# Attention weights of the first half batch kept in float32 and transposed on TensorE, with v scaled on GpSimd, two weight tiles loaded early and more slack in the plan

## Chip, cores and metric

One core of a Trainium2 chip runs the whole program. The metric is the device time of one execution in microseconds; lower is better. The inputs are four batches of eight heads, 576 rows and 64 columns for q, k and v, a number tau, and four weight matrices, all float32.

## What is computed

```python
scores = scale * np.matmul(q, k.transpose(0, 1, 3, 2))
thresh = np.max(scores, axis=-1, keepdims=True) - tau
scores = np.where(scores >= thresh, scores, -1000000000.0)
scores = scores - np.max(scores, axis=-1, keepdims=True)
attn = np.exp(scores)
attn = attn / (np.sum(attn, axis=-1, keepdims=True) + 1e-09)
attn_out = np.matmul(attn, v)                     # (4, 8, 576, 64)
x = attn_out.transpose(0, 2, 1, 3).reshape(2304, 512)
h = x @ w1_in;  x = (h * np.clip(h + 3, 0, 6) / 6) @ w1_out
h = x @ w2_in;  out = (h - np.tanh(h)) @ w2_out   # hidden width 2048
```

## The kernel before, in words

**The order.** Nothing is issued where it is written. Each step is a `Task` with an engine, an estimated duration and a due time (`key`), recorded with `add`; buffers are `Buf`s of a `Ring`, from which the dependences follow. `Plan.issue` then plays the estimates through and issues, on each engine, the ready task with the smallest due time; `slack` makes a task ready later than its estimate. So every engine has a fixed list, worked off in order, and a changed estimate or due time moves neighbours in all lists.

**Attention.** A unit is one head's 128 query rows against all 576 keys (`softmax`, line 577 on). There are 144 units: per batch 16 in a first half (`g` = 0, row chunks 0 and 1 of each head), then 16 and four units of left-over rows. A unit is four score products on TensorE (128x288, line 577), the row maximum on VectorE (582), the exponential on ScalarE (584), the threshold (587 or 590) and the masking on VectorE (593), which leaves the unnormalised weights `e` in float32. Two units of a head make a pair. For a pair, ScalarE copies `e` to float16 (`pp`, 598), GpSimd writes the rest that float16 lost beside it (602), SP's queue sends one transposing DMA of 18 blocks (`pt`, 605), and `weighted` multiplies on TensorE: 14 float16 products of 65 columns per unit with v (628), and ScalarE takes the result (635). Column 65 of v holds ones, so the row sum comes along. v itself is scaled to a power of two and split into two float16 parts in `v_round` (525 to 543: ScalarE twice more, TensorE once, VectorE three small steps, GpSimd). `k_round` and `q_round` transpose k and q on TensorE and split them.

**First layer.** Its first half of hidden columns runs beside attention, per half batch: `x_round` normalises and transposes, `layer1` multiplies (`mm3`, line 388, and line 734). Each weight matrix is loaded in tiles of 512 KB by `load_w`, and each tile is split into a high and a low part: absolute value on ScalarE (358), four VectorE steps (a clamp, 361, then 363, 366, 369), a copy on ScalarE (376) and a subtraction on GpSimd (378). For the 16 tiles of this first half (`WA`) the working buffer `wu` of these steps is a PSUM tile `m`; for the 48 tiles of the other halves (`weights`) it is in SBUF. The PSUM ring `R_m` (two tiles) also holds the products of `layer1`.

**After attention.** The second half of the first layer, then the second layer over nine blocks of 256 rows (`hidden`). In the second layer's first two blocks GpSimd forms the low part of each gated tile (701), between the subtractions of the weight tiles of its second half (378).

## Time and profile before

| | us |
|---|---|
| runs: median (lowest to highest) of three | 1147.84 (1145.71 to 1150.57) |
| profiled execution, its time | 1146.78 |
| its span | 1144.7 |
| TensorE busy in the span | 1073.2 (94%) |
| VectorE | 718.4 (63%) |
| ScalarE | 616.5 (54%) |
| GpSimd | 419.0 (37%) |

The span is what the profiler sees of the execution; its own time is 2.1 us longer. The shares are averages over stages that differ, so the rows further down split the span into stretches. Engines are named PE (TensorE), DVE (VectorE), ACT (ScalarE), POOL (GpSimd) and SP in them, L and a number is the line of the kernel, `out<-in` are the tiles, and PEclk is TensorE's granted clock as a share of 2.4 GHz.

### The profile page before, as it was taken

Reading aid. Unit: us, or ns where it says so; the run is one execution under the profiler, and the core shown is the slowest. Engines: PE = TensorE matmul, PEld = TensorE weight load, DVE = VectorE, ACT = ScalarE, POOL = GpSimd, SP = SyncE. Lnnn points to the kernel's source line nnn. Section 1 sums busy time; section 2 is a strip of 40 time slices with the busy share of each in tenths; the row PEclk is TensorE's granted clock in tenths of the full one; section 3 lists DMA queues with packets and bytes.
Section 4 is the critical chain, followed back from the end, with each engine's and each line's share of the span. In section 5 each row is a group of like instructions: output and inputs, shape, how many; then the busy total and the mean of one; then the engine's idle time right before and its main releaser. Section 6 shows DMA issues by size and latency. Waiting matters only on the chain.

```text
span 1144.7 us, 23228 instructions
## 1 busy us (share of the span) xinstructions
PE 1073.2 (94%) x9104; PEld 1002.1 (88%) x9104; DVE 718.4 (63%) x1365; ACT 616.5 (54%) x1268; POOL 419.0 (37%) x420
## 2 busy tenths in 40 slices
PE   5668899999999999889999999989999999999998
PEld 4557788998999899889999999978999999999997
DVE  6889887678777867587865663995323333333232
ACT  6868888689677867445544443544323323323222
POOL 3666767667656765652412210465200000000000
PEclk8668899999999999999999999999999999999999
DMA  7889678777977787778633430241100000000000
GB/s 186 180 190 230 131 183 156 173 148 188 164 168 144 167 155 129 210 198 282 184 93 94 129 94 1 76 131 33 38 1 19 1 19 19 1 19 20 1 20 19
DMA packets 257454, 125.77 MB, mean 110 GB/s; under 512 B 200257, under 2 KB 250945, under 8 KB 257345
## 3 DMA queue, kind: packets, MB, share of 16 engines
q1 hardware_dynamic: 247296, 114.72, 43.0%
q0 software_dynamic: 9504, 9.44, 3.6%
q8 instruction: 72, 1.18, 0.4%
q14 instruction: 38, 0.30, 0.1%
q10 hardware_dynamic: 544, 0.13, 0.1%
HBM read 62.92 MB, written 18.87 MB: 71 GB/s over the span
## 4 chain that ended last, share of the span: by engine, by line
PE 74%; DVE 8%; issue 5%; ACT 5%; POOL 3%; DMA 3%; SPq 0%; POOLq 0%; DVEq 0%; ACTq 0%
PE ya L388 24%; PE m L388 18%; PE h L388 12%; PE s L577 7%; PE m L734 6%; PE tp L628 5%; DVE e L593 2%; PE tp L460 2%; POOL bi L378 1%; DVE z L582 1%; ACT e L584 1%; POOL g L701 1%; DMA pt<-pp 1%; DMA st<-in_moe_w_in_dram 1%; DVE st L369 1%
## 5 line engine op out<-in xcount | busy, mean ns | idle before, releaser
L602 POOL TENSOR_TENSOR pp<-e,pp 128x128 f16<-128x128 f32 (+3 forms) x160 | 185.4, 1179 | 119.3 <-ACT pp L598 58.3
L698 ACT ACTIVATE g<-t 128x256 fp32r<-128x256 f32 x216 | 90.0, 417 | 103.8 <-DVE t L905 78.2
L582 DVE TENSOR_REDUCE z<-s 128x1 f32<-128x576 f32 x144 | 108.2, 753 | 53.3 <-PE s L577 52.4
L701 DVE TENSOR_TENSOR g<-t,g 128x256 fp32r<-128x256 f32 x184 | 92.9, 505 | 71.9 <-PE ya L388 44.6
L593 DVE SCALAR_TENSOR_TENSOR e<-s,z,e 128x576 f32<-128x576 f32 x144 | 116.1, 811 | 15.6 <-ACT e L584 9.9
L388 PE MATMUL m<-xT,ai 128*128 128x256 f32 (+1 forms) x768 | 121.7, 304 | 3.7 <-DVE t L693 2.5
L577 PE MATMUL s<-ks,q 128*128 128x288 f32 x512 | 105.2, 334 | 17.2 <-DVE e L593 16.5
L388 PE MATMUL ya<-ao,g 128*128 128x512 f32 x432 | 113.7, 396 | 5.8 <-POOL g L701 4.8
L388 PE MATMUL ya<-g,bo 128*128 128x256 f32 x864 | 116.1, 283 | 2.0 <-DVE g L701 1.9
L584 ACT ACTIVATE e<-s,z 128x576 f32<-128x576 f32 x144 | 105.4, 738 | 23.3 <-DVE z L582 18.3
L388 PE MATMUL h<-x,bi 128*128 128x256 f32 x864 | 115.4, 283 | 0.1
L388 PE MATMUL m<-x,bi 128*128 128x256 f32 x864 | 115.1, 283 | 0.0
L388 PEld LDWEIGHTS h<-x,bi 128*128 128x128 f32 x864 | 111.0, 191 | 3.3 <-POOL bi L378 0.3
L388 PEld LDWEIGHTS m<-x,bi 128*128 128x128 f32 x864 | 111.0, 191 | 3.0
L388 PEld LDWEIGHTS m<-xT,ai 128*128 128x128 f32 x768 | 107.9, 192 | 6.0 <-DVE t L693 3.5
L388 PEld LDWEIGHTS ya<-g,bo 128*128 128x128 f32 x864 | 108.9, 192 | 2.8 <-DVE g L701 2.5
L388 PE MATMUL ya<-bo,g 128*128 128x512 f32 x432 | 111.2, 393 | 0.0
L577 PEld LDWEIGHTS s<-ks,q 128*128 128x128 f32 x512 | 81.7, 210 | 24.4 <-issue 9.3
L628 PE MATMUL tp<-vt,pt 128*128 128x65 f16 (+1 forms) x2240 | 87.9, 199 | 8.1 <-DMA pt<-pp 4.5
L388 PEld LDWEIGHTS ya<-ao,g 128*128 128x128 f32 x432 | 75.9, 189 | 21.1 <-POOL g L701 7.8
L628 PEld LDWEIGHTS <-pt 128*128 128x128 f16 (+1 forms) x2240 | 79.7, 104 | 16.3 <-DMA pt<-pp 6.5
L905 DVE TENSOR_TENSOR t<-h,t 128x256 f32<-128x256 f32 x72 | 30.4, 423 | 98.8 <-ACT t L903 98.8
(101 smaller groups left out, 1825.2 us busy)
## 6 DMA issues: line engine op xcount, KB each, us to landing
st<-in_moe_w_in_dram SPq DMA_DIRECT2D x32, 512.0 KB, 3.9
st<-in_moe_w_out_dram SPq DMA_DIRECT2D x32, 512.0 KB, 4.0
x<-xs POOLq DMA_DIRECT2D x18, 512.0 KB, 5.4
xs<-xT SPq DMA_DIRECT2D x8, 640.0 KB, 4.8
y<-ys SPq DMA_DIRECT2D x9, 512.0 KB, 8.9
kr<-in_k_dram SPq DMA_DIRECT2D x16, 256.0 KB, 3.1
vr<-in_v_dram SPq DMA_DIRECT2D x16, 256.0 KB, 3.6
xs<-xT SPq DMA_DIRECT2D x8, 512.0 KB, 4.5
```

The source lines that it names most:

```text
L388: nc.tensor.matmul(ps, l[a], r[b], start=first and t == 0 and i == 0, stop=last and t == 2 and i == n - 1,)
L460: nc.tensor.transpose(ps[:, o:o + w], s.rearrange("p r d -> p (r d)"), ident[p0:p0 + w, p0:p0 + w])
L577: nc.tensor.matmul(ps.t[:, half, 0:SH], l, ks[:, half * SH:(half + 1) * SH], start=i == 0, stop=i == len(ops) - 1,)
L582: add("dve", 0.69, key, lambda: nc.vector.tensor_reduce(out=z.t[:, 0:1], in_=s(), axis=AX.XY, op=ALU.max, negate=True), r=[ps], w=[z])
L584: exp = add("act", 0.66, key, lambda: nc.scalar.activation(out=ex(), in_=s(), func=ACTF.Exp, bias=z.t[:, 0:1]), r=[ps, z], w=[e])
L593: add("dve", 0.74, key, lambda: nc.vector.scalar_tensor_tensor(out=ex(), in0=s(), scalar=z.t[:, 1:2], in1=ex(), op0=ALU.is_ge, op1=ALU.mul ...
L602: add("pool", t_pool(w * (src.stop - src.start)), key, lambda src=src, dst=dst: nc.gpsimd.tensor_tensor(out=pp.t[:, 0:w, dst], in0=e.t[:, ...
L628: nc.tensor.matmul(pv.t[0:m, w_ * (D + 1):(w_ + 1) * (D + 1)], pt.t[:, n, blk, rows], vv, start=o == 0, stop=o == len(ops) - 1)
L698: hi = add("act", t_act(n, sbuf=True), key, lambda: nc.scalar.activation(out=gh(), in_=t(), func=ACTF.Copy), r=[bt], w=[bh])
L701: add(low, t_pool(n) if low == "pool" else t_dve(n), key, lambda: eng.tensor_tensor(out=gl(), in0=t(), in1=gh().bitcast(F32), op=ALU.subtr ...
L734: prev = [add("pe", t_mm(n, 1), kd, lambda p=p, l=l, r=r, m=m, s=s, ps=ps: nc.tensor.matmul(ps.t[:, 0:n], W["o", m].t[:, l, s], r[m].t[:, ...
L905: add("dve", t_dve(n), key, lambda: nc.vector.tensor_tensor(out=s_(), in0=p(), in1=s_(), op=ALU.subtract), r=[ps, t], w=[t])
```

## The change

For the first half of batch 0 (`plain`, 16 of 144 units), the weights `e` stay float32. TensorE transposes them in four blocks per unit into a PSUM tile of `R_m`, and the 64 left-over columns of both units of a pair into another tile; ScalarE copies both to SBUF, in the memory that `pt` and `pp` had. `weighted32` multiplies them, five float32 products per unit, with v as loaded (`load_v32`, three loads per pair of heads and a column of ones; the memory is that of weight tiles not yet needed). These eight pairs have no float16 copy, no GpSimd subtraction and no transposing DMA. The split of v of batch 0 is due only before its second half. For all v, the scaling by the power of two goes from ScalarE to GpSimd.

In `load_w` the absolute value is always written to SBUF, and the clamp is done there; for the first eight tiles (`low`) by GpSimd. The next step reads SBUF and writes the PSUM tile, which is therefore taken later. The first two tiles are asked for on ScalarE's queue without slack. k is due one unit later (`LK`), the tiles of the second layer's second half every 4 us in place of 3 (`W2S`), and the split steps of the later tiles get slacks of 0.1 to 0.3 us.

```diff
-    LK, LQ, LV, LD = 5, 3, 1, 4
+    LK, LQ, LV, LD = 4, 3, 1, 4
+    CB, CC, CD = 0.1, 0.3, 0.2
-    W2B, W2S = 6.0, 3.0
+    W2B, W2S = 6.0, 4.0
+    NCL = 8
...
-        wst, wu, W = R_st.new(), (scratch or R_wu).new(), R_w[name, kind, m].new()
+        wst, wu, W = R_st.new(), R_wu.new(), R_w[name, kind, m].new()
+        sc = scratch.new() if scratch else wu
+        mid = lambda dt: sc.t.bitcast(dt)
+        eng, sync = ("act", nc.scalar) if queue else ("dma", nc.sync)
...
+        def clamp():
+            (nc.gpsimd if low else nc.vector).tensor_scalar(
+                out=part(F32), in0=part(F32), scalar1=TINY, scalar2=HUGE, op0=ALU.max, op1=ALU.min)
...
+        if low:
+            add("pool", t_pool(DM), key + 3, clamp, r=[wu], w=[wu], slack=cs)
+        else:
+            add("dve", 0.5, key + 3, clamp, r=[wu], w=[wu], slack=cs)
         steps = [
-            lambda: nc.vector.tensor_scalar(
-                out=part(F32), in0=part(F32), scalar1=TINY, scalar2=HUGE, op0=ALU.max, op1=ALU.min),
             lambda: nc.vector.tensor_scalar(
-                out=part(I32), in0=part(I32), scalar1=3, scalar2=0x3FFFFFF8,
+                out=mid(I32), in0=part(I32), scalar1=3, scalar2=0x3FFFFFF8,
...
-        add("act", t_act(N, sbuf=True, scalars=True), key, lambda: nc.scalar.activation(
-            out=raw(), in_=raw(), func=ACTF.Copy, scale=sv.t[:, 2 * j:2 * j + 1]), r=[vr, sv], w=[vr])
+        add("pool", t_pool(N), key, lambda: nc.gpsimd.tensor_scalar(
+            out=raw(), in0=raw(), scalar1=sv.t[:, 2 * j:2 * j + 1], scalar2=None, op0=ALU.mult), r=[vr, sv], w=[vr])
...
-        if u == us[-1]:
+        if plain(b, g):
+            transpose32(u, key, e, pp, pt, n, len(us))
+        elif u == us[-1]:
...
+    def transpose32(u, key, e, pp, pt, n, count):
+        tp = R_m.new()
+        def tr():
+            for i in range(NC):
+                nc.tensor.transpose(tp.t[:, i * 128:(i + 1) * 128], e.t[:, n, i * 128:(i + 1) * 128], ident)
+        add("pe", NC * 0.11, key, tr, r=[e], w=[tp])
+        add("act", t_act(SM), key, lambda: nc.scalar.activation(
+            out=blocks32(pt)[:, n].rearrange("p k n -> p (k n)"), in_=tp.t, func=ACTF.Copy), r=[tp], w=[pt])
+        if n == count - 1:
+            tl = R_tp.new()
+            def left():
+                for i in range(count):
+                    nc.tensor.transpose(tl.t[0:LF, i * 128:(i + 1) * 128], e.t[:, i, SM:S], ident)
+            add("pe", count * 0.11, key, left, r=[e], w=[tl])
+            add("act", t_act(count * 128), key, lambda: nc.scalar.activation(
+                out=left32(pp), in_=tl.t[0:LF, 0:count * 128].rearrange("p (u n) -> p u n", u=count),
+                func=ACTF.Copy), r=[tl], w=[pp])
+    def weighted32(u, key):
...
+                for i, cb in enumerate(ORDER):
+                    nc.tensor.matmul(out, blocks32(pt)[:, n, i, :], vv[:, h % 2, cb, :], start=i == 0, stop=False)
+                nc.tensor.matmul(out, left32(pp)[:, n, :], vv[0:LF, h % 2, NC, :], start=False, stop=True)
...
-                rounds.append((u - LV, ("v", b, j)))
+                rounds.append((first_unit[b, 1, j] - LV if plain(b, g) else u - LV, ("v", b, j)))
...
-                    "a", kind, m, w1_in if kind == "i" else w1_out, 0, T0 + STEP * (W0 + WS * n + WO * (kind == "o")), 0.8, slack=ST, scratch=R_m, cs=CS)
+                    "a", kind, m, w1_in if kind == "i" else w1_out, 0, T0 + STEP * (W0 + WS * n + WO * (kind == "o")), 0.8, slack=ST if n > 1 else 0.0, scratch=R_m, cs=CS, queue=n < 2, low=n < NCL)
```

**TensorE, the first pair of units.** Before, the first products with v (`vt`, `pt`) follow the scores (`s`) of eight units and the transposes of left-over q rows:

```order
L577 MATMUL s<-ks,q 128x288 x8
L476 MATMUL tp<-ident,left 64x64 x2
L460 MATMUL tp<-ident,left 128x64 x2
L577 MATMUL s<-ks,q 128x288 x8
L628 LDWEIGHTS pt
L628 MATMUL tp<-vt_94,pt 128x65
```

Now (`m<-ident,e` and the 64-row `tp<-ident,e` are the new transposes, `v_126` is v as loaded):

```order
L609 MATMUL s<-ks,q 128x288 x4
L668 MATMUL tp<-ident,e 64x128 x2
L658 MATMUL m<-ident,e 128x128 x4
L686 MATMUL tp<-v_126,pt 128x65 x4
L687 MATMUL tp<-v_126,pp 128x65
L686 MATMUL tp<-v_126,pt 128x65 x4
L687 MATMUL tp<-v_126,pp 128x65
L609 MATMUL s<-ks,q 128x288 x4
```

The 28 pairs of a weight load and a product are ten products, the transposes stand between the scores, and the first products follow the scores of four units, the last of which is the first row here.

**VectorE, the first weight tile.** Before, its clamp (361) and shift (363) work in the PSUM tile `m`, behind three small steps for v:

```order
L531 TENSOR_SCALAR vs<-tp 128x1
L533 TENSOR_SCALAR vs<-vs 128x1
L536 RECIPROCAL sv<-vs 128x2
L485 TENSOR_TENSOR ks<-tp,ks 64x2x64
L361 TENSOR_SCALAR m<-m 128x512
L593 SCALAR_TENSOR_TENSOR e<-s,z,e 128x576
L363 TENSOR_SCALAR m<-m 128x512
```

Now the shift (376) reads `wu` in SBUF and comes right behind the first maximum:

```order
L614 TENSOR_REDUCE z<-s 128x1
L376 TENSOR_SCALAR m<-wu 128x512
L517 TENSOR_TENSOR ks<-tp,ks 64x2x256 x2
L625 SCALAR_TENSOR_TENSOR e<-s,z,e 128x576
L614 TENSOR_REDUCE z<-s 128x1
L517 TENSOR_TENSOR ks<-tp,ks 64x2x64
L379 SCALAR_TENSOR_TENSOR m<-st,m 128x512
```

The clamp of this tile has left VectorE's list, and its other three steps stand 16 to 18 places earlier.

**GpSimd, second layer.** Before, from the first weight tile (`bi`) of the second half, with the low parts `g`:

```order
L378 TENSOR_TENSOR bo_11069<-st,bo_11069 128x512
L701 TENSOR_TENSOR g<-t,g 128x256
L378 TENSOR_TENSOR bi_11103<-st,bi_11103 128x512
L701 TENSOR_TENSOR g<-t,g 128x256
L378 TENSOR_TENSOR bo_11150<-st,bo_11150 128x512
L701 TENSOR_TENSOR g<-t,g 128x256 x2
```

Now, at the same tiles:

```order
L391 TENSOR_TENSOR bo_11085<-st,bo_11085 128x512
L787 TENSOR_TENSOR g<-t,g 128x256
L391 TENSOR_TENSOR bi_11128<-st,bi_11128 128x512
L787 TENSOR_TENSOR g<-t,g 128x256 x2
L391 TENSOR_TENSOR bo_11182<-st,bo_11182 128x512
L787 TENSOR_TENSOR g<-t,g 128x256
```

Over the 16 tiles 21 of the 32 low parts stand between subtractions now, 18 before.

## Rows read from the trace of the kernel before

**Rows 1.** Table of stretches: busy time (instructions) per engine, granted clock, DMA share, GB/s.
```profile
core 0: us, PE busy (x) PEld busy (x) DVE busy (x) ACT busy (x) POOL busy (x), PEclk, DMA share, GB/s
...
131.40:200.00 68.60, 64.64 (x740) 61.09 (x739) 52.26 (x91) 55.37 (x115) 47.02 (x46) 0.98 0.79 161
...
720.00:800.00 80.00, 74.19 (x478) 65.68 (x477) 65.51 (x98) 38.33 (x83) 45.01 (x40) 1.00 0.27 86
...
20.00:100.00 80.00, 56.67 (x474) 47.93 (x474) 71.99 (x120) 62.51 (x120) 51.77 (x47) 0.65 0.87 187
20.00:131.40 111.40, 80.89 (x732) 70.00 (x733) 102.31 (x173) 91.38 (x184) 73.64 (x70) 0.73 0.86 184
```

**Rows 2.** Groups of VectorE by shape: total, mean ns; then idle time before, releaser.
```profile
L593 DVE SCALAR_TENSOR_TENSOR e<-s,z,e 128x576 f32<-128x576 f32 x144 | 116.1, 811 | 15.6 <-ACT e L584 9.9 <-ACT z L587 3.9
L582 DVE TENSOR_REDUCE z<-s 128x1 f32<-128x576 f32 x144 | 108.2, 753 | 53.3 <-PE s L577 52.4
...
L361 DVE TENSOR_SCALAR wu<-wu 128x512 f32<-128x512 f32 x48 | 29.0, 604 | 9.5 <-ACT wu L358 8.5
```

**Rows 3.** Waits of VectorE and TensorE, 20 to 131.4 us: total, times, longest.
```profile
DVE z L582 <- PE s L577: 2.8, 9, 0.8
...
PE s L577 <- DVE e L593: 18.4, 13, 4.9
```

**Rows 4.** Line 361, the clamp: duration min/median/max ns, first and last start.
```profile
L361 DVE TENSOR_SCALAR wu<-wu x48: 408/426/2416, 462.0 to 780.7; 128x512 f32<-128x512 f32 x48
L361 DVE TENSOR_SCALAR m<-m x16: 681/690/700, 23.2 to 127.2; 128x512 f32<-128x512 f32 x16
```

**Rows 5.** Chain that ended last: start, us, what.
```profile
48.81 1.58 PE tp L628 x28
...
114.23 1.88 PE tp L628 x56
119.32 2.91 PE m L388 x24
```

**Rows 6.** TensorE's instructions in order of time: start, duration, line, count.
```profile
4.98 1.09 PE L460 MATMUL tp<-ident,kr 128*128 128x128 f32 x4 [4.98 <-DMA kr<-in_k_dram]
5.86 1.06 PE L460 MATMUL tp<-ident,qr 128*128 128x128 f32 x4
...
116.67 0.60 PE L460 MATMUL tp<-ident,qr 128*128 128x128 f32 x4
117.02 1.65 PE L388 MATMUL m<-xT,ai 128*128 128x256 f32 x12
...
119.05 0.28 PE L527 MATMUL tp<-vs,ones 128*128 128x1 f32 x2
119.19 3.05 PE L388 MATMUL m<-xT,ai 128*128 128x256 f32 x24
```

**Rows 7.** Groups of all engines by shape.
```profile
L602 POOL TENSOR_TENSOR pp<-e,pp 128x1024 f16<-128x1024 f32 x64 | 137.3, 2146 | 0.0
...
L598 ACT ACTIVATE pp<-e 128x1152 f16<-128x1152 f32 x64 | 74.2, 1160 | 8.3 <-DVE e L593 8.1
...
L543 POOL TENSOR_TENSOR vt<-vr,vt 128x640 f16<-128x640 f32 x16 | 21.8, 1362 | 11.2 <-ACT vt L541 11.2
...
L483 ACT ACTIVATE ks<-tp 64x512 fp32r<-64x512 f32 x32 | 18.9, 589 | 4.9 <-PE tp L460 4.6
...
L539 ACT ACTIVATE vr<-vr,sv 128x640 f32<-128x640 f32 x16 | 13.2, 827 | 1.4 <-DVE sv L536 1.0
```

**Rows 8.** Table of stretches, near the start; last column GB/s.
```profile
4.00:6.00 2.00, 1.02 (x5) 0.99 (x6) 0.54 (x5) 0.00 (x0) 0.40 (x1) 1.00 1.05 265
```

**Rows 9.** Waits of TensorE, 560 to 900 us.
```profile
PE ya L388 <- POOL g L701: 4.8, 7, 0.9
PE ya L388 <- ACT g L698: 1.1, 1, 1.1
```

More of the change, by code (lines that the diff above doesn't have):

```diff
@@ L40, in t @@
         if self.tile is None:
[L41 removed]
+            self.tile = self.make() if self.slot is None else self.make(self.slot)
         return self.tile
@@ L50, in __init__, with new @@
         self.slots = [0.0] * n
-    def new(self):
-        b = Buf(self, self.bufs[-self.n] if len(self.bufs) >= self.n and not self.free else None)
+    def new(self, make=None):
+        b = Buf(self, self.bufs[-self.n] if len(self.bufs) >= self.n and not self.free else None, make)
         self.bufs.append(b)
@@ L272, in attention_moe_moe_kernel @@
     ones = at_p.tile([128, 128], F32, name="ones")
+    ones_h = at_p.tile([128, H], F32, name="ones_h")
     def ring(pool, n, shape, dt, name, **kw):
@@ L331, in attention_moe_moe_kernel, with load_w @@
     w_rings(slot0, "io", "a")
-    def load_w(name, kind, m, src, half, key, step, after=(), slack=0.0, scratch=None, cs=0.0):
-        wst, wu, W = R_st.new(), (scratch or R_wu).new(), R_w[name, kind, m].new()
+    def load_w(name, kind, m, src, half, key, step, after=(), slack=0.0, scratch=None, cs=0.0, queue=None, low=None):
+        wst, wu, W = R_st.new(), R_wu.new(), R_w[name, kind, m].new()
+        sc = scratch.new() if scratch else wu
         f0 = half * FH + m * 128
@@ L410, in attention_moe_moe_kernel @@
     NU = len(units)
-    KR, QR, VR, KL, QL, KS, VT, SV, QT = ({} for _ in range(9))
+    KR, QR, VR, KL, QL, KS, VT, SV, QT, V32 = ({} for _ in range(10))
+    plain = lambda b, g: (b, g) == (0, 0)
     def load_k_left(b, key):
@@ L616, in weighted @@
             XT[xi] = R_x.new() if h is not None else R_xl.new()
-        xt = XT[xi]
+        if plain(b, g):
+            return weighted32(u, key)
+        us, vt, pv, xt = sum_group(u), VT[b, j], R_tp.new(), XT[xi]
         work = [(slice(0, 128), h % 2, n) for n in range(len(us))] if h is not None else [
@@ L657, in x_round @@
             cs, sv = 2 if i == 0 else 1, SV[b]
+            scales = (lambda: ones_h) if plain(b, g) else (lambda: sv.t)
             def invert():
@@ L804, in attention_moe_moe_kernel @@
         pend = {}
+        for (b, g, j), u in first_unit.items():
+            if plain(b, g):
+                load_v32(b, j, when(u + 1) - LD * STEP)
         for u in range(NU + LAG + XL + 4):
@@ L863, in attention_moe_moe_kernel, with weights @@
         PM = t_mm(NB, 3 * KD)
-        def weights(half, rings_, w_in, w_out, key, step, after=lambda n: ()):
+        def weights(half, rings_, w_in, w_out, key, step, cs, after=lambda n: ()):
             W = {}
@@ L910, in attention_moe_moe_kernel @@
         late = pend[NU - WBU].writers[-1:]
-        WB = weights(1, {"i": "b", "o": "b"}, w1_in, w1_out, start - FW + WBO, WBS, lambda n: late)
+        WB = weights(1, {"i": "b", "o": "b"}, w1_in, w1_out, start - FW + WBO, WBS, CB, lambda n: late)
         key = T2
```

63 lines of the change are left out of this document (47 added, 16 removed).

## The prediction, made before the changed kernel ran

> **What bounds the kernel now.** I read the table of stretches first [rows 1]. TensorE is busy 64.64 of 68.6 us after 131.4 us and stays so to the end, so a microsecond is won there only by giving TensorE less to do or by filling its gaps. Up to 131.4 us it is otherwise: between 20 and 131.4 us TensorE works 80.89 of 111.4 us, 30.5 us are idle, and its granted clock is 0.73 on average, 0.65 up to 100 us, that is about 1.2 GHz for some 70% of that part and 2.4 GHz for the rest. The engine that is full there is VectorE: 102.31 of 111.4 us, 9.1 us idle. ScalarE has 91.38 and GpSimd 73.64 us. I end the stage at 131.4 us because VectorE starts the last clamp of the first layer's 16 weight tiles at 127.2 us [rows 4], and the tile's three other steps of 0.69 and some maskings fill the next four; behind that its load falls to 52.26 of 68.6 us. So the first stage lasts as long as VectorE's list, and what is taken off that list shortens it.
>
> VectorE's list per attention unit is the maximum and the masking, 0.753 and 0.811 us [rows 2]; each weight tile adds four steps, the first of 0.690 us in the form that works in PSUM [rows 4]. The waits show how little of VectorE's idle time TensorE causes: 2.8 us in 9 waits [rows 3].
>
> **The change, part by part.** *Clamps.* For 8 of the 16 tiles the clamp leaves VectorE for GpSimd: 8 x 0.690 = 5.5 us off VectorE. For the other 8 it works in SBUF in place of PSUM. The same line in SBUF has a mean of 604 ns over 48 later tiles [rows 2], so 8 x 0.086 = 0.7 us more comes off. Sum A: -6.2 us. The median there is 426 ns and the longest 2416, while the PSUM form never leaves 681 to 700 [rows 4]: something stretches the SBUF form now and then. The Trainium skill, "SBUF — State Buffer", section "Who interferes with whom", says that VectorE in a two-port mode and GpSimd lock each other out of a shared port pair for a whole instruction. The spread in [rows 4] agrees; by that rule each of the 8 clamps waits for what GpSimd runs, 0.66 of the time (73.64/111.4) half of 2.146 us, so it costs 0.41 + 0.71 = 1.12 us and the term becomes 8 x 0.43 = +3.4 us, and the whole sum below would be 4.1 us less good, 1142.9 us. I stay with the mean of the rows, since it was taken beside a busy GpSimd too.
>
> *TensorE's new work.* For the 16 units of the first half batch the 14 float16 products go, and four transposes, one transpose of the rest (two per pair of units) and five float32 products come. Where the clock is full, 56 float16 products take 1.88 us on the chain, 0.034 each, and 24 layer products 2.91, 0.121 each; at half clock a float16 product takes 1.58/28 = 0.056 [rows 5]. Four transposes start at 116.67 and the next work at 117.02 us, 0.088 each; near the beginning, at 4.98 and 5.86, it is 0.22 [rows 6]. A float32 product of 65 columns stands nowhere. The only plain float32 product, of one column, shows two instructions, 0.14 us from start to next start [rows 6]. Bounds: two instructions at a transpose's 0.088, 0.175 us; twice that, 0.35 us. I take 2 x (0.088 + 65 columns at 0.121/256 us) = 0.24 us, nearest to the one-column row. Per unit 5 x 0.088 + 5 x 0.24 - 14 x 0.034 = 1.17 us, for 16 units 18.7 us; bounds 13.5 and 27.5 us; all at half clock 16 x (5 x 0.22 + 5 x 0.48 - 14 x 0.056) = 43.4 us. It lies beside VectorE's list, in TensorE's 30.5 us. Cover gone, it costs what exceeds them.
>
> *Layer work ahead.* In the new order 151 first-layer products precede the 168th score product, before 120. 31 more at 0.121 us [rows 5] use TensorE's gaps in the first stage and are missing from the full stretch behind it. Term B: -3.8 us. Room: A shortens the stage to 105.2 us, which leaves 24.3 us idle for 18.7 + 3.8 = 22.5. It fits, barely, if the clock stays as it is, and easily if more work raises it: what ran at half clock up to 100 us is the larger part of 56.67 us of work [rows 1].
>
> *New waits.* A pair used to go ScalarE, GpSimd, a transposing DMA, TensorE. Now TensorE waits in order for VectorE's masked weights, ScalarE for the transposes, TensorE for ScalarE's copies, and the PSUM tiles of the casts are shared with the transposes. The scores of the next units stand behind these on TensorE, and VectorE behind the scores. The nearest row: VectorE waits 0.31 us per wait on scores [rows 3]. 16 such are 5.0 us, of which I take half: +2.5 us; bounds 0 and 10 (its own idle time doubled).
>
> *ScalarE, GpSimd, DMA.* Per pair of units ScalarE loses one copy of 1.160 us and gains two of 0.589 and a smaller one below that: at most +0.6 us, 8 pairs +5 us; each scaling of v that leaves takes 0.827 us away [rows 7]. About even, on an engine with 20 us of idle time. GpSimd loses 8 x 2.146 us and more, and gains 8 clamps and 16 scalings, each below the 1.362 us of the two-operand form [rows 7]: its idle 38 us cover that. SP issues 8 transposing DMAs fewer and 12 loads of v more. All this I cost at nothing; if ScalarE's cover went, the copies of the transposes would be late next, and TensorE's products behind them.
>
> *Start.* Two weight tiles, 1 MB, are now asked for by ScalarE at once, between the first q and k. At the 265 GB/s of the first transfers [rows 8] 1 MB is up to 4 us ahead of the second k; against that the first scaling of v (0.827 us on ScalarE) leaves the front. Bounds -0.8 and +4; I take +0.5, as the first k and q are asked for earlier.
>
> *Second layer.* Casts of its second half run beside 18 of GpSimd's 32 low parts before, beside 21 now. TensorE waits 4.8 us for these parts and 1.1 us for ScalarE's copies [rows 9], with VectorE 65.51 of 80 us busy [rows 1]. Casts spread over 21/18 of the time relieve it: I take a third, -2.0; bounds -5.9 and +2. The smaller slacks elsewhere and k one unit later swap neighbours only; nothing.
>
> Sum: -6.2 - 3.8 + 2.5 + 0.5 - 2.0 = **-9.0 us**. The profiled execution took 1146.8 us (span 1144.7 and 2.1 around it), so 1137.8; the median of the runs lies 1.1 higher, so I forecast **1138.9 us**.
>
> **Rivals.** *TensorE at half clock becomes the bound (slower).* If the clock stays low while the new work runs, TensorE needs 80.9 + 43.4 + 3.8 = 128.1 us where the stage has 111.4: +16.7, less the 3.8 done ahead, less 1.5 for layer two and the start: +11.4, **1159.2 us** against the median of the runs, as all times here. It is no gain from about 2.0 us of net new work per unit on ((30.5 + 1.5)/16), over 0.5% slower from 2.4. For it: between 20 and 100 us TensorE has 71% busy time and yet the half clock mostly [rows 1]. Against: the stretch after 131.4 us, 94% busy, shows 0.98 [rows 1], and a TensorE that becomes the bound would be such a stretch. The Trainium skill, "TensorE: Matmul & The Clock Gate", section "Part 4: PE-mode transpose", says that the full clock does not engage for transposes. No row here isolates that; by it this rival would hold, 1159.2 us, since a large part of the new work is transposes. Chance 0.13.
>
> *The gain is lost in new waits (no change).* Waits at 10 us in place of 2.5: 1146.3 us; with products at 0.35 us instead, TensorE needs 27.5 + 3.8 us against 30.5, the stage grows by 0.8, and with the 3.8 and the 1.5 1143.3 is left. For it: two engines nearly full, each waiting in order for the other. Against: TensorE's waits on VectorE, not the reverse, are the long ones before, 18.4 us [rows 3]. 1143 to 1150, chance 0.23. In this sense the change would not do what it says: the transposing DMA was hidden anyway.
>
> *More than forecast.* Half of VectorE's own 9.1 us goes (4.5), no new waits (2.5), the start gains 0.8 in place of losing 0.5, all 5.9 us of layer two go (3.9 more): **1126.6 us**, 1124 to 1131. For it: in SP's queue eight transposing DMAs no longer stand ahead of loads. Against: every idle place at once. Chance 0.12.
>
> **How the numbers follow.** The forecast has 0.52 and its own range 1130 to 1144 (waits, start and layer two at their nearer bounds). From 1128 to 1151 us, most of the half-clock case (0.11) and the lower part of the large gain (0.06) are left out. 0.5% is 5.7 us, about what a measurement of this kernel can tell from none: faster is below 1142.1, slower above 1153.6. Faster: 0.48 of the forecast and 0.12, together 0.60. Slower: 0.10 of the half-clock case and 0.02 of the lost gain, 0.12. The same: 0.28.
>
> **What would show it.** Right: the last first-layer weight step on VectorE near 121 to 125 us; VectorE still above 88% busy in the stage; TensorE's idle there nearly gone and its clock above 0.8; eight GpSimd clamps; the layer-two waits below 5 us; from there the same times shifted. Wrong: TensorE above 95% busy before 100 us at a clock near 0.6; float32 products above 0.35 us; VectorE idle 15 us or more behind the scores; the first maximum later than 13 us.

## The result, and the profile after

The change makes the kernel **slower**: 1162.26 us (median of four runs, 1160.34 to 1166.23) against 1148.46 us (four runs of before beside them), ratio 1.0126 with a 95% interval of 1.009 to 1.0162. The forecast was 1138.9 us, and 1162.26 lies 11.3 us above its range. The profiled execution of the change has a span of 1161.6 us, 16.9 more than before.

All of the loss lies in attention. The first view is what one line of VectorE, the row maximum, took, before and after: duration min/median/max in ns, first and last start.

```profile
L582 DVE TENSOR_REDUCE z<-s x144: 696/756/759, 11.7 to 460.1; 128x1 f32<-128x576 f32 x144
L614 DVE TENSOR_REDUCE z<-s x144: 695/757/760, 12.0 to 481.3; 128x1 f32<-128x576 f32 x144
```

The start is late by 0.3 us and the end by 21.2. Counting the maxima along the way shows where (end of the n-th, read from VectorE's instructions in order of time):

| n-th maximum | 4 | 8 | 12 | 20 | 40 | 140 |
|---|---|---|---|---|---|---|
| before, us | 22.5 | 34.3 | 48.0 | 73.2 | 149.6 | 449.1 |
| after, us | 26.2 | 40.6 | 60.6 | 94.2 | 162.2 | 471.0 |
| later by | 3.7 | 6.3 | 12.6 | 21.0 | 12.5 | 21.9 |

Some 21 us are lost in the first 20 units, the first 16 of which are the float32 half batch. Part of it is regained by the fortieth; from the 46th on the distance stays between 17 and 25 us. The table of stretches, to be held against [rows 1]:

```profile
core 0: us, PE busy (x) PEld busy (x) DVE busy (x) ACT busy (x) POOL busy (x), PEclk, DMA share, GB/s
131.40:200.00 68.60, 61.51 (x708) 57.53 (x707) 51.40 (x89) 54.16 (x115) 52.79 (x48) 0.95 0.71 153
720.00:800.00 80.00, 77.58 (x551) 72.15 (x550) 65.52 (x104) 38.28 (x83) 34.80 (x31) 1.00 0.26 82
20.00:100.00 80.00, 63.03 (x362) 55.89 (x362) 55.68 (x94) 52.96 (x115) 45.77 (x37) 0.76 0.48 130
20.00:131.40 111.40, 87.22 (x569) 78.41 (x570) 83.05 (x139) 76.29 (x165) 63.22 (x54) 0.77 0.58 149
44.00:52.00 8.00, 7.23 (x30) 6.69 (x31) 2.90 (x4) 3.26 (x9) 5.06 (x3) 0.50 0.07 23
36.00:40.00 4.00, 2.79 (x20) 2.20 (x18) 3.73 (x6) 3.96 (x10) 1.67 (x2) 1.00 0.72 165
```

VectorE is no longer full: busy 83.05 of 111.4 us, so it is idle for 28.4 us where it had 9.1. No other engine has taken its place: TensorE is idle 24.2 us and ScalarE 35.1. A stage in which every engine waits is held by a chain of waits. The waits of the same stretch (us in total, times, longest), against [rows 3]:

```profile
DVE z L614 <- PE s L609: 12.4, 8, 3.8
PE s L609 <- DVE e L625: 12.3, 6, 6.0
...
DVE e L625 <- ACT z L619: 9.9, 8, 3.1
...
DVE m L376 <- POOL wu L365: 3.5, 5, 1.1
```

VectorE's waits on scores have gone from 2.8 to 12.4 us, those on ScalarE's threshold are 9.9, and TensorE still waits 12.3 us for the masking. SP's queue, from 0 to 60 us, shows a wait that the kernel before did not have:

```profile
SPq L472 <- DMA v<-in_v_dram: 13.2, 4, 6.0
SPq L481 <- PE tp L492: 12.7, 1, 12.7
```

Line 472 loads the left-over rows of the float32 v. In SP's order of time (start, duration; L445 is k, L481 q, L469 the main blocks of v; the last row is the third k tile in the kernel before):

```profile
4.61 1.27 SPq L469 DMA_DIRECT2D v<-in_v_dram  x2
11.91 0.62 SPq L472 DMA_DIRECT2D v<-in_v_dram  x1
12.58 1.11 SPq L481 DMA_DIRECT2D qr<-in_q_dram  x2
13.73 1.23 SPq L469 DMA_DIRECT2D v<-in_v_dram  x2
17.41 0.62 SPq L472 DMA_DIRECT2D v<-in_v_dram  x1
18.08 0.60 SPq L469 DMA_DIRECT2D v<-in_v_dram  x1
18.73 0.62 SPq L445 DMA_DIRECT2D kr<-in_k_dram  x1
...
7.98 0.52 SPq L430 DMA_DIRECT2D kr<-in_k_dram  x1
```

SP issues the two main blocks, done at 5.88, and then stands until 11.91: the third load into the same tile waits for the second to land. q and k stand behind it. The third k tile is asked for at 18.73 us, where the kernel before asked at 7.98; its transposes run at 22.47, before at 16.65. Then TensorE, ScalarE, GpSimd and VectorE in order of time from 42 us on (some rows):

```profile
42.35 1.12 PE L658 MATMUL m<-ident,e 128*128 128x128 f32 x4 [0.36 <-DVE e L625]
...
43.79 0.66 ACT L369 ACTIVATE wu<-st 128x512 f32<-128x512 f32 x1 [1.71 <-DMA st<-in_moe_w_in_dram]
44.35 0.36 ACT L671 ACTIVATE pp<-tp 64x256 f32<-64x256 f32 x1
44.54 1.92 POOL L365 TENSOR_SCALAR wu<-wu 128x512 f32<-128x512 f32 x1 [2.78 <-ACT wu L369]
...
44.77 1.97 PE L686 MATMUL tp<-v,pt 128*128 128x65 f32 x8 [1.30 <-ACT pp L671]
...
46.67 0.69 PE L687 MATMUL tp<-v,pp 64*128 64x65 f32 x2
...
47.28 1.97 PE L686 MATMUL tp<-v,pt 128*128 128x65 f32 x8
...
49.80 1.12 PE L658 MATMUL m<-ident,e 128*128 128x128 f32 x4
...
50.99 1.31 PE L609 MATMUL s<-ks,q 128*128 128x288 f32 x4
...
52.34 0.76 DVE L614 TENSOR_REDUCE z<-s 128x1 f32<-128x576 f32 x1 [3.71 <-PE s L609]
```

This is the chain in one piece. ScalarE waits 1.71 us for a weight tile to land, and the small copy that TensorE needs (671) stands behind that. TensorE then multiplies two units at half clock (5 us), transposes, and only then computes scores, for which VectorE has waited 3.71 us. Ten microseconds earlier the same work ran at full clock:

```profile
34.12 1.11 PE L686 MATMUL tp<-v,pt 128*128 128x65 f32 x8
...
35.16 0.43 PE L687 MATMUL tp<-v,pp 64*128 64x65 f32 x2
...
37.08 0.66 PE L658 MATMUL m<-ident,e 128*128 128x128 f32 x4 [0.91 <-DVE e L625]
...
37.49 0.78 PE L609 MATMUL s<-ks,q 128*128 128x288 f32 x4
```

From start to next start four products (eight records) take 1.04 us here and 1.90 there.

Prices, for [rows 2, 4, 7] (total us, mean ns | idle before), first in the 400 us from the start, then over the whole run; the idle time before the masking (L625) was 15.6 us [rows 2]:

```profile
L571 POOL TENSOR_SCALAR vr<-vr,sv 128x640 f32<-128x640 f32 x14 | 26.5, 1892 | 10.6 <-DVE sv L568 9.3 <-ACT t L828 1.1
...
L365 POOL TENSOR_SCALAR wu<-wu 128x512 f32<-128x512 f32 x8 | 15.4, 1923 | 14.8 <-ACT wu L369 14.8
...
L365 DVE TENSOR_SCALAR wu<-wu 128x512 f32<-128x512 f32 x8 | 4.7, 592 | 0.1
```
```profile
L614 DVE TENSOR_REDUCE z<-s 128x1 f32<-128x576 f32 x144 | 107.6, 753 | 52.8 <-PE s L609 51.7
L625 DVE SCALAR_TENSOR_TENSOR e<-s,z,e 128x576 f32<-128x576 f32 x144 | 116.1, 813 | 35.3 <-ACT z L619 17.4
```

In the second layer TensorE's busy time from 720 to 800 us is 77.58 us, before 74.19, and its wait for GpSimd's low parts, 4.8 us before [rows 9], has halved (580 to 920 us):

```profile
PE ya L401 <- POOL g L787: 2.4, 3, 0.9
```

### The profile page after: what moved, and what is told of

Read it like the earlier page. It is cut to its first block, busy times and chain, and to the rows that moved or that the text cites. A ratio compares the mean times of both kernels' runs of the same rounds, so it can differ in the third digit from the quotient of the medians.

```text
span 1161.6 us, 23227 instructions
## 1 busy us (share of the span) xinstructions
PE 1090.6 (94%) x9120; PEld 1020.9 (88%) x9120; DVE 715.8 (62%) x1358; ACT 607.0 (52%) x1268; POOL 444.0 (38%) x432
## 4 chain that ended last, share of the span: by engine, by line
PE 77%; DVE 8%; DMA 4%; ACT 3%; POOL 3%; issue 3%; SPq 1%; POOLq 0%; DVEq 0%; ACTq 0%
PE ya L401 25%; PE m L401 19%; PE h L401 13%; PE s L609 6%; PE m L820 6%; PE tp L713 5%; DVE e L625 2%; PE tp L492 1%; DMA st<-in_moe_w_in_dram 1%; DVE z L614 1%; DVE wu L379 1%; DMA pt<-pp 1%; POOL wu L365 1%; DVE ks L517 1%; PE tp L686 1%
## 5 line engine op out<-in xcount | busy, mean ns | idle before, releaser
L636 POOL TENSOR_TENSOR pp<-e,pp 128x128 f16<-128x128 f32 (+3 forms) x144 | 165.4, 1170 | 76.2 <-ACT pp L632 52.3
L625 DVE SCALAR_TENSOR_TENSOR e<-s,z,e 128x576 f32<-128x576 f32 x144 | 116.1, 813 | 35.3 <-ACT z L619 17.4
L609 PE MATMUL s<-ks,q 128*128 128x288 f32 x512 | 101.2, 325 | 14.1 <-DVE e L625 14.0
L609 PEld LDWEIGHTS s<-ks,q 128*128 128x128 f32 x512 | 79.0, 203 | 18.6 <-DVE e L625 12.5
L401 PEld LDWEIGHTS ya<-bo,g 128*128 128x128 f32 x432 | 76.6, 189 | 13.9 <-POOL g L787 1.3
L820 PE MATMUL m<-gh,ao 128*128 128x256 f32 (+1 forms) x512 | 82.3, 299 | 2.2 <-DVE t L779 2.2
```

The lines of the kernel that those rows point to most:

```text
L401: nc.tensor.matmul(ps, l[a], r[b], start=first and t == 0 and i == 0, stop=last and t == 2 and i == n - 1,)
L609: nc.tensor.matmul(ps.t[:, half, 0:SH], l, ks[:, half * SH:(half + 1) * SH], start=i == 0, stop=i == len(ops) - 1,)
L625: add("dve", 0.74, key, lambda: nc.vector.scalar_tensor_tensor(out=ex(), in0=s(), scalar=z.t[:, 1:2], in1=ex(), op0=ALU.is_ge, op1=ALU.mul ...
L636: add("pool", t_pool(w * (src.stop - src.start)), key, lambda src=src, dst=dst: nc.gpsimd.tensor_tensor(out=pp.t[:, 0:w, dst], in0=e.t[:, ...
L820: prev = [add("pe", t_mm(n, 1), kd, lambda p=p, l=l, r=r, m=m, s=s, ps=ps: nc.tensor.matmul(ps.t[:, 0:n], W["o", m].t[:, l, s], r[m].t[:, ...
```

## The experiments

Four theories. **1**: TensorE's added time is the bound. **2**: SP's queue, held by the loads of v, and the early weights delay the start. **3**: GpSimd's clamps and scalings hold the casts. **4**: the new in-order waits between the engines. All results, with the start of the last maximum in each profile:

| kernel | median us | ratio to before | last maximum us |
|---|---|---|---|
| before | 1146.78 to 1148.46, beside each | 1 | 460.1 |
| the change | 1162.26 | 1.0126 (1.009 to 1.0162) | 481.3 |
| two products | 1161.73 | 1.0123 (1.0107 to 1.0139) | 480.0 |
| no float32 | 1157.62 | 1.0096 (1.0083 to 1.0109) | 474.3 |
| only float32 | 1176.7 | 1.0257 (1.0244 to 1.027) | 485.4 |
| before, later settings | 1141.62 | 0.9959 (0.9944 to 0.9974) | 460.3 |
| v apart | 1157.81 | 1.0083 (1.0063 to 1.0104) | 475.3 |
| no early weights | 1168.17 | 1.0176 (1.0156 to 1.0196) | 483.9 |
| transposes later | 1181.68 | 1.0299 (1.0282 to 1.0316) | 500.2 |
| planner's costs | 1166.52 | 1.017 (1.0141 to 1.02) | 483.6 |
| v apart, two products | 1152.67 | 1.004 (1.0026 to 1.0054) | 470.7 |
| no float32, GpSimd as before | 1161.46 | 1.0125 (1.0108 to 1.0142) | 474.6 |
| v apart, GpSimd as before | 1166.67 | 1.016 (1.014 to 1.0179) | 483.9 |
| v apart, two products, one transpose | 1151.14 | 1.0029 (1.0014 to 1.0044) | 466.1 |
| later settings, early weights | 1147.64 | 1.0006 (0.9996 to 1.0016) | 464.8 |
| later settings, k later | 1151.36 | 1.0032 (1.0022 to 1.0042) | 466.4 |
| later settings, early weights, SBUF clamp | 1155.98 | 1.0079 (1.0056 to 1.0102) | 476.4 |
| v apart, k as before | 1162.35 | 1.013 (1.011 to 1.0149) | 481.1 |
| v apart, k as before, PSUM clamp | 1168.64 | 1.0184 (1.016 to 1.0207) | 482.9 |
| v apart, PSUM clamp | 1160.69 | 1.0117 (1.0098 to 1.0137) | 479.2 |

Differences below are taken between ratios, times 1147 us, about the median of before.

**Large parts first.**

*Two products.* The order of every engine stays.

```diff
-                for i, cb in enumerate(ORDER):
+                for i, cb in enumerate(ORDER[:1]):
```

> The changed kernel, with the float32 products of the first half batch cut from five to two per unit (the other three 128-row blocks of weights are left out of the sum); every transpose, copy, load and the order stay. 48 products go, 0.26 us each at full clock and 0.48 at half clock in the profile of the change: 12.5 to 23 us of TensorE's work before 100 us. Theory 1 (TensorE's added work at half clock is the bound between 36 and 100 us): 10 to 18 us faster than the change, 1144 to 1152 us. Theory 2 (SP's queue, held by loads of v, and the early weights set the start) and theory 3 (GpSimd's clamps of 1.92 us and scalings of 1.88 us hold the casts): the products lie beside that, under 4 us, 1158 to 1163 us.

No gain (0.3 us), as theories 2 and 3 expected: in the change as it is, TensorE's time is not what the end waits for. The eighth maximum ends no earlier (40.9 us for 40.6), the twentieth and the fortieth do, by 4.2 and 3.2 us (90.0 for 94.2, 158.9 for 162.2), but of that 0.6 us are left at the hundredth. What takes the gain back, far behind the float32 half batch, was not found.

*No float32, and only float32.*

```diff
-    plain = lambda b, g: (b, g) == (0, 0)
+    plain = lambda b, g: False
```

> The changed kernel with the float32 path switched off: clamps and scalings on GpSimd, early weights, the slacks and the spread casts of layer two all stay. Theory 1 (TensorE's added work): the whole loss of 20 us goes and the 5 us of layer two stay: 1137 to 1144 us. Theory 2 (SP's queue): the loads of v go as well, so only the early weights are left: 1140 to 1150 us. Theory 3 (GpSimd): it has 8 clamps of 1.92 us, the scalings, and the low parts of the weights back, so it is worse off than in the change: 1152 us or more.

The other way round, the float32 path alone on the kernel before (with the `load_w` of before, scalings on ScalarE, `LK` 5, no early weights, settings as before).

> The kernel before with the float32 path alone: no clamp and no scaling on GpSimd, no early weights, the settings of layer two as before. Theory 1 (TensorE's added work): the loss of about 20 us in the first 20 units stays and the 5 us of layer two go: 1162 to 1172 us. Theory 2 (SP's queue): the loads of v are there, the early weights are not: 1153 to 1162 us. Theory 3 (GpSimd): clamps and scalings are gone from it, so most of the loss goes: 1148 to 1154 us.

Theory 1 missed both ways: without float32 the kernel is still 11.0 us slow (where theory 3 expected it, so GpSimd is tried below), and float32 alone costs 29.5 us, more than the whole change. The parts do not add up: the rest of the change takes back some 15 us of what float32 costs, and costs 11 where float32 is absent. The two losses lie in different places. Without float32 the twentieth maximum is 3.1 us late and the thirtieth 1.8, but the fortieth 14.2 (163.9 us for 149.6): this loss falls between 112 and 164 us, for the most part behind the stage that the prediction looked at.

*The later settings alone.*

```diff
-    W2B, W2S = 6.0, 3.0
+    CB, CC, CD = 0.1, 0.3, 0.2
+    W2B, W2S = 6.0, 4.0
...
-            (key - T2) / 16, lambda n
+            (key - T2) / 16, CC, lambda n
```

> The kernel before with nothing but the change's settings of the later weight tiles (slacks of their casts, steps of layer two's second half 4 instead of 3 us apart). If the 4.9 us that layer two took less in the profile of the change come from these settings: 1142 to 1146 us. If they come from the attention's other order: 1147 to 1150 us, no difference.

A gain of 4.7 us, all of it from these settings (the spacing and the slacks were not run apart). Attention is untouched (last maximum 460.3), and the second layer looks like that of the change:

```profile
720.00:800.00 80.00, 77.63 (x510) 70.32 (x509) 69.00 (x105) 40.34 (x89) 45.58 (x41) 1.00 0.28 86
```
```profile
PE ya L389 <- POOL g L702: 2.4, 3, 0.9
```

The change has the same gain in a stage of its own, so its attention loses some 19 us. This kernel beats both.

**SP's queue.** *v apart*: the third load goes to addresses that the second does not come near.

```diff
-                out=at32()[0:LF, :, NC, 0:D], in_=v[b, hs, SM:S, :]
+                out=left()[0:LF, :, 0:D], in_=v[b, hs, SM:S, :]
...
+        left = lambda: flat(3 * NC, 3 * NC + 2).rearrange("p (h d) -> p h d", h=2)
```

> The changed kernel, with the left-over rows of the float32 v in an address range apart from the two main blocks of the same tile, so that SP no longer holds the third load of each tile until the second has landed (13.2 us of SP's waits in four loads in the profile of the change, the longest 6.0). The order of every engine stays. Theory 2 (SP's queue delays the first k and q, and the delay is kept): the fourth unit comes 3 to 6 us earlier and the time falls by as much, 1155 to 1159 us. Theory 4 (what decides is the new order on TensorE, in which transposes and products stand ahead of the scores of the next units): the early gain is taken back by unit 20, 1160 to 1164 us.

Theory 2 holds for the loads: 4.9 us back. The intervals of the two ratios overlap a little, but none of the four runs took longer than 1158.4 us and none of the change less than 1160.34. The order on every engine is the same; SP now runs through:

```profile
4.56 1.27 SPq L470 DMA_DIRECT2D v<-in_v_dram  x2
5.87 0.63 SPq L473 DMA_DIRECT2D v<-in_v_dram  x1
6.54 2.02 SPq L483 DMA_DIRECT2D qr<-in_q_dram  x2
...
12.94 0.54 SPq L445 DMA_DIRECT2D kr<-in_k_dram  x1
```

The fourth maximum ends at 23.1 us (26.2 in the change, 22.5 before), the twelfth is 5.9 us earlier than in the change, and the last starts at 475.3, 6.0 earlier: what is won at the start is kept to the end. The third k tile is still asked for 5 us later than before, since the loads of the float32 v stand ahead of it in the queue.

*No early weights.*

```diff
-  slack=ST if n > 1 else 0.0, scratch=R_m, cs=CS, queue=n < 2, low=n < NCL)
+  slack=ST, scratch=R_m, cs=CS, low=n < NCL)
```

> The changed kernel, with its first two weight tiles asked for by SP in their old places and with the old slack, not by ScalarE at the start. Theory 2 (1 MB ahead of k and q delays the start): 2 to 4 us faster, 1157 to 1160 us. Theory 4 (the order on TensorE): no gain, 1160 to 1166 us, or a loss of some us, since the casts of two tiles then come later, in the stage in which VectorE waits.

5.7 us slower (the intervals just overlap): the early weights do not delay the change, they help it. That half of theory 2 falls.

**TensorE once the queue is free.** *v apart, two products* takes both edits above.

> The changed kernel with the left-over rows of v apart (as in the run before it, 1157.8 us) and the float32 products cut from five to two per unit (three of the four 128-row blocks of weights are left out of the sum). In the profile with v apart TensorE is busy 36.5 of the 40 us between 40 and 80 us, at a granted clock of 0.76. Theory 1 in its later form (once the start is freed, TensorE's added time is the bound there): 48 products of 0.26 to 0.48 us go, of which some 6 to 12 us shorten the stage, 1146 to 1152 us. Theory 4 (the order and the waits between the engines decide): under 2 us, 1156 to 1159 us.

Now 4.9 us come back, 0.7 us short of theory 1's range and far outside theory 4's, with the order of every engine as it was. VectorE's waits on scores in the stage fall from 14.2 us (the longest 4.0) to 8.4 (1.7). *One transpose*: three of the four are left out as well.

```diff
-            for i in range(NC):
+            for i in range(1):
                 nc.tensor.transpose(tp.t[:, i * 128:(i + 1) * 128], e.t[:, n, i * 128:(i + 1) * 128], ident)
```

> As the run with v apart and two products (1152.7 us), and with one float32 transpose per unit in place of four (the copy repeats the one block four times, so three blocks of weights are left out). 48 transposes of 0.10 to 0.22 us go from TensorE, 5 to 10 us. If TensorE's time is what is left of the loss: unit 20 near 77 to 79 us in place of 82, and 1147 to 1150 us. If it is the waits of the engines on each other: 1151 to 1154 us, unit 20 at 81 to 82 us.

1.3 us less, with overlapping intervals: the transposes' time is not told apart from nothing. The two signs named beforehand disagree: the time is that of waits, the twentieth maximum, at 78.6 us for 81.8, that of TensorE's time. The three kernels in the table of stretches, 20 to 131.4 us, one row each in the order v apart, two products, one transpose:

```profile
20.00:131.40 111.40, 91.05 (x650) 82.65 (x648) 88.99 (x151) 82.22 (x177) 68.04 (x58) 0.80 0.55 142
```
```profile
20.00:131.40 111.40, 87.32 (x629) 76.03 (x629) 95.67 (x163) 88.47 (x191) 74.89 (x64) 0.79 0.60 153
```
```profile
20.00:131.40 111.40, 89.85 (x599) 77.57 (x598) 97.28 (x165) 89.37 (x195) 76.53 (x66) 0.67 0.61 153
```

VectorE's idle time goes 28.4 (the change), 22.4, 15.7, 14.1 us; before it was 9.1.

**GpSimd.** Clamps on VectorE, scalings on ScalarE, on the kernel without float32 and on the one with v apart.

```diff
-    NCL = 8
+    NCL = 0
...
-        add("pool", t_pool(N), key, lambda: nc.gpsimd.tensor_scalar(
+        add("act", t_act(N, sbuf=True, scalars=True), key, lambda: nc.scalar.activation(
```

> The changed kernel without the float32 path (1157.6 us so far), and now with the clamps of the weights on VectorE and the scalings of v on ScalarE again; early weights, slacks and layer two's settings stay. Theory 3 (without the float32 path, GpSimd is the bound, busy 69.2 of the 80 us from 20 to 100 us; 8 clamps of 1.92 and scalings of 1.88 us hold it): 1138 to 1144 us, below both kernels. If the loss of that kernel came from the early weights or the slacks instead: 1152 to 1158 us.

> The changed kernel with the left-over rows of v apart (1157.8 us so far), and with clamps on VectorE and scalings on ScalarE. Theory 3 for the change as it is (GpSimd's clamps and scalings hold the casts, and these the units): 1150 to 1154 us. Theories 1 and 4 (TensorE's time or order; GpSimd has room since the low parts of the weights are gone, 48.6 of 80 us): no gain, 1157 to 1164 us, VectorE having 8 steps more.

Theory 3's gain comes in neither: 3.3 us slower (the intervals just overlap) and 8.8 us slower, both times also beyond the other expected range. This shows that the work is no cheaper on VectorE and ScalarE. It does not show that GpSimd's time is free: without float32 VectorE's busy time from 20 to 131.4 us rises by it from 93.34 to 101.29 us, and in the change GpSimd's clamps are 6.9% of the chain that ended last by 140 us. What the first shows besides is the price of the clamp in SBUF (0 to 200 us):

```profile
L365 DVE TENSOR_SCALAR wu<-wu 128x512 f32<-128x512 f32 x16 | 16.0, 1002 | 1.5 <-ACT wu L369 1.3
```

1.002 us, against 0.592 in the change and 0.690 in PSUM [rows 4]. The means hide two cases. In the change seven of the eight clamps take 0.42 to 0.43 us and one takes 1.79; it starts inside one of GpSimd's subtractions (L636), which is the second row:

```profile
99.66 1.79 DVE L365 TENSOR_SCALAR wu<-wu 128x512 f32<-128x512 f32 x1
99.04 2.13 POOL L636 TENSOR_TENSOR pp<-e,pp 128x1024 f16<-128x1024 f32 x1
```

The clamp ends at 101.45 us, 0.28 us behind the end of the subtraction. In the kernel of the 1.002 us nine of the 16 clamps start inside such a subtraction, and each ends 0.28 us behind it, after 0.57 to 2.33 us. Beside GpSimd's scaling (L571), which has one input, a clamp took 0.42 us.

**The order.** Two kernels with the change's work in another order: slack on the transposes, and measured costs.

```diff
-        add("pe", NC * 0.11, key, tr, r=[e], w=[tp])
+        add("pe", NC * 0.11, key, tr, r=[e], w=[tp], slack=2.0)
```

> The changed kernel, with 2.0 us of slack on the float32 transposes, so that in TensorE's order the scores of up to three more units stand ahead of them and of their products; the work is the same. Theory 4 (the loss is the in-order chain: TensorE waits for the masked weights before its transposes, and VectorE for the scores behind transposes and products, 12.4 us of waits on scores): a third to all of it comes back, 1148 to 1157 us. Theory 1 (TensorE's added time itself): no change beyond 3 us, 1159 to 1165 us. Theory 2 (SP's queue): no change either, since the loads stand where they stood.

```diff
-        add("pe", 1.1 * len(us), key, products, r=[pt, pp, v32], w=[pv, xt])
+        add("pe", 2.3 * len(us), key, products, r=[pt, pp, v32], w=[pv, xt])
```

> The changed kernel, whose planner is given the costs that the profile shows at half clock for the new work: products of a unit 2.3 us in place of 1.1, a float32 transpose 0.22 in place of 0.11, a clamp on GpSimd 1.92 in place of 1.2, a scaling 1.9 in place of 1.5. The work is the same, the order is another. Theory 4 (an order built on costs at full clock puts too much ahead of the scores): 4 to 12 us faster, 1150 to 1158 us. Theories 1 and 2 (amount of TensorE's work, SP's queue): 1159 to 1166 us.

Both missed, by a loss of 19.8 and 5.0 us against the change (the second with overlapping intervals). With the transposes later VectorE's waits on scores are longer, where the change has 12.4 us, 8 and 3.8:

```profile
DVE z L614 <- PE s L609: 18.1, 12, 8.3
```

Products of two pairs now follow each other on TensorE (42.57 to 52.63 us), and the scores come behind them all. A later place takes a wait away only if nothing as long takes it. Theory 4 is not refuted as a mechanism (here the waits grow with the time, and with v apart three products less take 5.8 us off them and 4.9 off the time), but no run takes the waits away alone; as a recipe it failed.

**The smaller parts, on the kernel before with the later settings.** Early weights; `LK` 4 for 5; early weights and the clamp in SBUF on VectorE (16 tiles).

> The kernel before with the change's settings for the later weight tiles (1141.6 us) and, of the rest of the change, the early weights alone: two tiles asked for by ScalarE at the start. If early weights give VectorE work where it is idle, as the change without them was 6 us slower: 1136 to 1140 us. If they are what makes the change without float32 and without GpSimd's new work slow: 1150 to 1160 us.

> The kernel before with the settings of the later weight tiles (1141.6 us), and k prepared 4 units ahead in place of 5, as in the change. I costed this at nothing: 1140 to 1144 us. If it is what makes the change without float32 and without GpSimd's new work slow: 1148 to 1160 us.

> As the run before it but one (later settings and early weights), and with the clamps of the first layer's tiles on VectorE in SBUF, as the second 8 tiles of the change have them. In the kernel without float32 and without GpSimd's new work these clamps took 1.118 us on average, where the form in PSUM takes 0.690, beside a busy GpSimd: 16 x 0.43 = 6.9 us more on VectorE, which is the full engine there. If that rule of the port holds: 4 to 8 us slower than the same kernel with the clamps in PSUM. If the mean of the later tiles held (0.604): 1 us faster.

Each costs: 5.4, 8.4 and a further 8.4 us. The first result lies between its two expectations; the second is the expected one for a cost; the third is 0.4 us beyond the range for the rule of the port. The SBUF clamp again took longer than in PSUM:

```profile
L366 DVE TENSOR_SCALAR wu<-wu 128x512 f32<-128x512 f32 x16 | 15.6, 975 | 2.9 <-ACT wu L363 2.8
```

16 x (0.975 - 0.690) = 4.6 us of VectorE's time explain about half of that. Last, the same parts undone on the change with v apart: `LK` 5, that with the PSUM clamp for the 8 tiles on VectorE, and the PSUM clamp alone.

> The changed kernel with the left-over rows of v apart (1157.8 us), and with k prepared 5 units ahead again. If k one unit later costs the change what it costs the kernel before (9.7 us): 1147 to 1151 us. If that cost hangs on the other work around it: 1155 to 1161 us.

> As the run before it, and the 8 clamps that stay on VectorE back in PSUM. In the changed profile the SBUF form took 0.88 us on average before 100 us, the PSUM form 0.69: 8 x 0.19 = 1.5 us off VectorE, which is not full here: up to 3 us faster than the run before it. If the form costs what it cost in the kernel without float32 (0.99 against 0.69 us there, 8.3 us of time for 16): 3 to 5 us faster.

> The changed kernel with the left-over rows of v apart (1157.8 us), k 4 units ahead as in the change, and the 8 clamps that stay on VectorE back in PSUM: 1 to 3 us faster, 1155 to 1157 us, if 8 x 0.19 us are all they cost; 3 to 5 us faster, 1153 to 1155 us, by half of the 8.3 us that 16 cost in the kernel without float32.

All slower than with v apart: 5.4, 11.6 and 3.9 us (the last with intervals that just overlap), and all outside what was expected. The 0.88 us of the last two expectations are the mean of three clamps; over all eight of the change it is 0.592, below the 0.690 of the PSUM form, so there was no time of VectorE to win. The same edit, k one unit later, costs 8.4 us on one kernel and saves 5.4 on the other.

## Why the prediction was wrong

**The step that failed: "So the first stage lasts as long as VectorE's list", and what followed from it, "It lies beside VectorE's list" of TensorE's new work and "All this I cost at nothing" of ScalarE, GpSimd, DMA and SP.** In the change VectorE is idle for 28.4 of the stage's 111.4 us, in large part behind two queues that work in order. The first is SP's. The prediction counted its "12 loads of v more" and stopped there; four of them each hold the queue, 13.2 us in all, with k and q behind: 4.9 us, shown by the run with v apart. The second is TensorE's, below. The start was costed at +0.5 with +4 as its upper bound, by the bytes of the early weights; the delay came from another cause, and the early weights are a gain in the change (5.7 us), though they cost 5.4 on the kernel before.

**New waits, +2.5 with bounds 0 and 10.** The bound was VectorE's own idle time doubled; it rose from 9.1 to 28.4 us. The price was taken from waits that exist before, 0.31 us each. One of the new ones is 3.71 us, because two units' products at half clock stand in it. Of the 19.3 us of added idle time, 6.0 go with SP's holds and 6.7 with three products of five.

**TensorE's new work.** At full clock the estimate was right: 1.04/4 = 0.26 us a product against 0.24 assumed. At half clock it is 1.90/4 = 0.48, above the bound of 0.35. It was taken as "beside VectorE's list". It isn't: it stands in one queue with the scores, and once SP is freed it costs 4.9 us.

**Clamps, -6.2.** The price in SBUF came out for the change, 0.592 us against 0.604, but by luck: it is the mean of seven short clamps and a long one. The gain could not come, since VectorE is not the bound any more. Where it is nearly full, in the kernels without float32, the term has the wrong sign: the clamps in SBUF cost 8.4 us, and GpSimd with 8 of them and the scalings takes 3.3 back. GpSimd's prices "below the 1.362 us" were wrong: 1.923 and 1.892; taking the work back made the change slower all the same. The Trainium skill, "SBUF — State Buffer", section "Who interferes with whom", gave the rule of the shared port pair from which the prediction worked out 1.12 us. The trace agrees: the clamps that start inside a subtraction of GpSimd (L636) end 0.28 us behind it. How many do so sets the mean: one of eight in the change, nine of 16 in the kernel without float32 and with GpSimd as before, which comes near the 1.12 us with 1.002.

**Layer work ahead, -3.8.** The lead is there and passes: 151 first-layer products for 120 before the 168th score product, but 204 for 216 before the 200th. At the end it is not seen: the last maximum is late by 21.2, the end by 16.9, and the 4.3 us between are no more than what the later settings give (4.7).

**Layer two, -2.0 (bounds -5.9 and +2).** Right in sign, and larger: -4.7, by the settings alone. The wait that was to shrink shrank by 2.4 us; where the other 2.3 come from is not shown. **k one unit later, "nothing"**: 8.4 us on the kernel before, and its undoing costs 5.4 on the change; "swap neighbours only" was no argument.

**The rivals.** *Half clock becomes the bound* gave the sign and nearly the number, 1159.2, but not the mechanism: TensorE is idle 24.2 us in the stage, its clock there rose from 0.73 to 0.77, and two products of five alone change nothing (0.3 us); that the number was near is luck. *The gain is lost in new waits* comes nearest to the mechanism, with a price that ended too early. Of the signs of being wrong the float32 products above 0.35 us came (0.48), VectorE's waits on scores fell short of the 15 us (12.4), and a TensorE above 95% busy and a first maximum later than 13 us did not come. The Trainium skill, "TensorE: Matmul & The Clock Gate", section "Part 4: PE-mode transpose", says that the full clock does not engage for transposes. The trace differs in so far as they run at the full clock where it is granted: four start at 37.08 and the next work at 37.49 us, 0.10 each, in a stretch at 1.00. Whether transposes help to raise the clock no run here tells.

**The sum, as far as it is shown**, from before: later settings -4.7, SP's holds +4.9, products +4.9, transposes 1.3 (not told apart from nothing). That leaves 14.5 + 4.7 - 4.9 - 4.9 - 1.3 = 8.1 us. What it is made of stays open by this way of counting.

The runs allow another one, in which the parts are added to the kernel before one after the other:

| added, in this order | us | forecast |
|---|---|---|
| later settings | -4.7 | -2.0 |
| early weights | +5.4 | +0.5 |
| clamps of all 16 tiles in SBUF, on VectorE | +8.4 | with the row after next: -6.2 |
| k one unit later | +5.3 | 0 |
| 8 clamps and all scalings on GpSimd | -3.3 | see above |
| the float32 path | +3.4 | -3.8 + 2.5 |
| together | +14.5 | -9.0 |

Each row is the difference of two kernels in the table of results; in the last two rows the intervals of the two kernels overlap. (With k, the planner's estimate for a clamp also changes, from 0.65 to 0.5 us.) In this order the clamps are the largest miss and the float32 path costs little; with v apart it is even 1.5 us faster than no float32, again with overlapping intervals. But these are not prices of the parts: float32 alone costs 29.5 us on the kernel before. Early weights, `LK` and the clamp's form each cost 5 to 8 us on the kernel before and save 4 to 6 on the change, with or without v apart. Each reorders the lists of all engines, so no run undoes one of them without moving the others, and why they change sign stays open. A kernel in which the order is fixed and one of these alone is changed was not tried.

## What to carry to other kernels

A load costs its queue the time it waits, not only its bytes: look up what a second and third load into one tile wait for, and what is queued behind. Work put into an idle engine is free only if nothing that another engine waits for stands behind it; in an in-order list look at its longest run at the slower clock (here 5 us of products ahead of the scores). Where a planner sets the order, try the parts alone, before and after each other: here one part was worth 4.7 us alone and hidden by a loss of some 19, and others cost on one kernel what they saved on the other.

## What was not expected of the hardware

TensorE was busy 7.23 of 8 us from 44 to 52 us at a granted clock of 0.50 (1.2 GHz), before that at 1.00 from 36 to 40 us with 2.79 of 4 us busy; a fuller engine did not have the higher clock. In between it was busy for less than half of the time, and there the clock fell; from 46 to 54 us it had no gap and the clock was still the lower one:

```profile
40.00:44.00 4.00, 1.89 (x8) 0.90 (x6) 3.07 (x7) 2.29 (x7) 0.40 (x1) 0.66 0.92 293
46.00:54.00 8.00, 8.00 (x35) 7.44 (x35) 2.84 (x4) 2.51 (x6) 4.89 (x4) 0.50 0.00 1
```

It is not the float32 work alone: in the kernel before the same 44 to 52 us have 7.37 us busy at 0.51.

A load whose destination did not overlap that of the load before it, only lay between its rows, waited for it to land all the same (5.88 to 11.91 us), and no longer did when it was moved away. Whether the program or the chip asks for this wait was not looked into.

VectorE's clamps in SBUF that started inside one of GpSimd's subtractions (L636) ended 0.28 us behind it; one that started inside GpSimd's one-input scaling took its usual 0.42 us.
